# A gated mix of infinite attention and a spectral filter on one core: four-group score units, a semaphore between GpSimd and VectorE, whole gate exponentials, and a new written-out order

## The chip, the cores and the metric

The kernel runs on one core of a Trainium2 chip. The core has TensorE (PE, matrix multiplication into PSUM), VectorE (DVE), ScalarE (ACT), GpSimd (POOL), SyncE (SP, which issues most transfers) and 16 DMA engines. The metric is device microseconds of one execution; a kernel's time is the median of several runs. Lower is better.

## The reference

Two branches work on the same input x of 2048 tokens by 640 columns, in bf16, and a gate mixes them.

```
g = sigmoid((x * gate_w).sum(-1))                     # one number per token
a = attention(x) @ wo                                 # 32 heads of 20, 4 segments of 512 tokens
b = irfft2(rfft2(x) * (w_r + 1j*w_i))               # 2-D spectral filter over 2048 x 640
out = g*a + (1-g)*b
```

The mix is what the kernel returns; both branches read the same x. In attention, each segment of 512 tokens has causal softmax attention within itself, and from the second segment on also reads a memory: `phi(q) @ M / (phi(q) @ z)`, where `phi(t)` is `t+1` above zero and `exp(t)` elsewhere, and M and z sum `phi(k)^T v` and `phi(k)` of the segments before. A sigmoid of beta weighs the two per head.

## The kernel before

**Attention.** Heads are taken in eight groups of four, so that a head's 20 rows stand in a 32-row quarter of the PE array. A segment has four pairs of groups. Scores are computed transposed (keys on partitions) and only where the causal mask leaves something, in *units*: kind 0 is the first key block against 512 queries, kind 1 the second and third key block, kind 2 the rest (128 columns for each head of a group). A unit takes all four banks of the PSUM pool "qk"; there is one unit in those banks at a time. `qk_unit` (L1306) records the matmuls of a unit, one ScalarE exponential out of the four banks into the SBUF tile `ex` (L1343), and GpSimd `affine_select` operations that zero the masked corners (`mask`, L1361, recorded at L1364). `UNITS` lists, for each pair of groups, which units are made: kinds 0 and 1 for each group alone, kind 2 for both groups at once. `pv_flipped` (L1257) multiplies the values with a group's finished exponentials in the first three segments, `pv_group` does it in the last. `ex` has three slots of 5120 elements per partition, used in turn by the groups.

**Memory.** `mem_read_tile` (L1216) makes half a tile of 128 tokens: three matmuls of `phi(q)` with `Mz` into one PSUM bank, then on DVE a denominator (L1231), its reciprocal (L1234) and the multiplication out of PSUM (L1236, L1239 for the last segment). `dn` is a ring of four small buffers between these.

**Gate.** The gate's dot product is a 641st column of the value projection. `v_part` copies that one column from PSUM by DVE (L1192) into `gl`: one copy where the key order is plain, two of 64 partitions each where the halves are swapped. `gate` (L1073) then makes one ScalarE exponential of the four columns of a segment (L1080) and small operations after it.

**Spectral branch.** `fft` makes five matmul stages, F1, D, T, Tb and Db, with DVE multiplying by the weights between T and Tb (L1526). Db, the last (stationary tile Cp, moving tile big), makes 16 blocks in two parts each; DVE adds the parts into G (L1568).

**End.** `finish_tile` normalizes the stored attention (L1609), adds the memory part to it (L1617) and multiplies by `wo` and by the gate.

**The order.** Everything is first *recorded* as operations with what they read and write; nothing is emitted at that point. `ORDER`, a list of numbers written out in the file, then gives the order of all operations: number v means operation v // 2, on the first or second engine that it can run on, v % 2. It is made by a planner that is not in the file. `Sched.schedule` replays this list with a small model of times, only to choose PSUM banks and semaphores and to add the waits that follow from them; the order on each engine is the list's. `Sched.emit` turns dependences into semaphore waits. Each engine works its own list in order, so that an operation that waits holds up all behind it on its engine.

PE's 128 by 128 array can be divided: into column pieces of 64 or 32 (an operation recorded with mode -1 or -2 may be emitted whole or split into such pieces, by what stands before it; split matmuls have line L546, whole ones L548), into two row halves, or into four row quarters by two column halves, as scores use it. The planner's table `COST` charges for each change between such divisions.

DVE operations with two operands in SBUF, or in its fast modes, are recorded with `lock=True`: the planner takes them to use a port that GpSimd also uses. In its model a locked DVE operation begins when GpSimd is free, GpSimd begins when the locked operation ends, and with `TIE` a locked operation that had to wait loses some more time to the next mask. None of that is a wait in the emitted program: before, no semaphore orders the two engines for the port.

The SBUF is nearly full, which is why buffers are laid over others with `at=`.

Of the kernel before, what the change touches and what calls it, by code (L numbers as in the profile page):

```python
# [49 lines left out]
class Sched:  # L50
    HOP = 70.0
    TIE = 0.15
# [62 lines left out]
    def schedule(self, pools, order, nsem=56):  # L115
# [33 lines left out]
        tied = [False]  # L149
# [26 lines left out]
        def head(e):  # L176
# [22 lines left out]
            if e == "dve" and o.lock:  # L199
                tied[0] = free["pool"] > t  # L200
                t = max(t, free["pool"])
            elif e == "dve":
                tied[0] = False
            elif e == "pool":
                t = max(t, port)
            return t

        while len(self.order) < len(order):
# [38 lines left out]
            if e == "dve" and o.lock:  # L247
                port = t + occ
# [247 lines left out]
class Kern:  # L496
# [80 lines left out]
    def dma(self, dst, src, nbytes, r, w, prio, tr=False, name="", after=(), queue="sp"):  # L577
# [34 lines left out]
    UNITS = (((0,), 0), ((0,), 1), ((1,), 0), ((0, 1), 2), ((1,), 1))  # L612
# [121 lines left out]
    def alloc(self):  # L734
# [54 lines left out]
        self.xn = T("xn", [P, 4 * D], at=self.ex.off + 2 * 10240)  # L789
        self.on = T("on", [P, 4 * D])  # L790
        self.mem = T("mem", [P, 4 * D])
# [508 lines left out]
    def exo(self, s, g):  # L1300
        return ((s * 8 + g) % self.NEX) * 5120
# [389 lines left out]
```

## Time and profile before

| what | value |
|---|---|
| median of 3 runs | 247.91 us (247.44 to 248.65) |
| the profiled execution's own time | 248.49 us |
| its span, first to last instruction | 246.4 us |
| mean granted TensorE clock | 0.985 |
| instructions | 10962 |
| DMA | 40.99 MB, mean 166 GB/s |

The page gives for each engine its busy time, its share of the span and its instructions; then the span in 40 equal slices of 6.16 us, one digit each, which is the busy share in tenths (9 is 90% or more); "PEclk" is in the same way the granted share of the TensorE clock. The chain of work that ended last is followed back from the last instruction: at each step to what released it, or to the instruction before it on its engine. A row of a group of instructions has the line, the engine, the operation, output and inputs with their shapes, the count, then busy time in us and the mean of one in ns, then the engine's idle time ahead of them and what ended it. A row that has three numbers with slashes gives the shortest, median and longest duration of one instruction in ns. A row of the time line has the start, the length, the engine and line, and how many instructions were merged in it.

### The profile page before, as it was taken

To read this page: it belongs to the slowest core of one execution; us is meant where nothing else is said; L and a number is where in the kernel's file an instruction comes from. 1 tells how busy PE (TensorE), PEld (TensorE's weight loads), DVE (VectorE), ACT (ScalarE), POOL (GpSimd) and SP (SyncE) were. 2 spreads that over 40 slices of the span, in tenths; PEclk is the share of its full clock that TensorE was granted. 3 is DMA by queue.
4 is the path that set the end of the run, shared out by engine and by line. 5 is a ranking of instruction groups with operands and counts; after the bars stand their busy time and mean duration, and the time that the engine had idled before them with its cause. 6 is when DMAs were issued, how large, how long until landed. Compare 5 with 4: busy or idle time off the path is not lost.

```text
span 246.4 us, 10962 instructions
## 1 busy us (share of the span) xinstructions
PE 230.1 (93%) x4691; PEld 136.0 (55%) x4705; DVE 205.6 (83%) x492; ACT 195.0 (79%) x222; POOL 163.8 (66%) x287
## 2 busy tenths in 40 slices
PE   7999989999889999999999999998989999999993
PEld 3544546565544454565555455555534666666882
DVE  0499889899899999798989988999996879986562
ACT  2588875999899999999899988999886788866120
POOL 8435295697686283889489485583869869688520
PEclk9999999999999999999999999999995999999999
DMA  7999206849063976887877895783576967634424
GB/s 223 318 349 191 74 13 142 238 112 197 32 167 103 191 200 150 182 211 208 226 147 197 243 243 134 195 223 122 169 189 153 242 155 148 98 83 96 136 53 105
DMA packets 54251, 40.99 MB, mean 166 GB/s; under 512 B 25404, under 2 KB 52028, under 8 KB 54204
## 3 DMA queue, kind: packets, MB, share of 16 engines
q1 hardware_dynamic: 52156, 38.89, 64.1%
q10 hardware_dynamic: 2048, 1.41, 2.2%
q8 instruction: 37, 0.61, 1.1%
q14 instruction: 10, 0.08, 0.1%
HBM read 21.94 MB, written 11.12 MB: 134 GB/s over the span
## 4 chain that ended last, share of the span: by engine, by line
PE 66%; DVE 23%; issue 4%; ACT 3%; DMA 1%; ACTq 1%; SPq 0%; DVEq 0%
PE psum L548 43%; PE psum L546 23%; DVE UV L1526 4%; DVE oU L1617 2%; DVE mem L1236 2%; DVE Cp L560 2%; DVE G L1568 2%; ACT ex L1343 2%; DVE va L1194 1%; DMA qkp<-qk_scr 1%; DVE Ac L560 1%; DVE Bt L560 1%; DVE dn L1234 1%; DVE ub L560 1%; DVE gate L1192 1%
## 5 line engine op out<-in xcount | busy, mean ns | idle before, releaser
L1364 POOL TENSOR_SCALAR_AFFINE_SELECT ex<-ex 128x256 bf16<-128x256 bf16 (+2 forms) x224 | 123.3, 574 | 51.8 <-ACT ex L1343 49.4
L1343 ACT ACTIVATE ex<-psum 128x2048 bf16<-128x2048 f32 (+4 forms) x92 | 138.6, 1506 | 13.4 <-PE psum L548 11.5
L548 PE MATMUL psum<-qkp 20*64 20x64 bf16 (+5 forms) x1024 | 31.9, 268 | 1.4 <-ACT ex L1343 0.8
L548 PE MATMUL psum<-xT,wq 128*32 128x512 bf16 (+1 forms) x212 | 27.8, 380 | 0.5 <-ACT xT L558 0.2
L1526 DVE TENSOR_TENSOR UV<-psum,Wt 128x642 bf16<-128x642 f32 x32 | 25.1, 820 | 1.7 <-PE psum L548 1.5
L546 PE MATMUL psum<-wv,xT 128*32 128x321 bf16 (+3 forms) x320 | 23.0, 302 | 1.0 <-DVE pkn L1069 1.0
L548 PE MATMUL psum<-xT,wk 128*32 128x512 bf16 (+1 forms) x194 | 23.2, 380 | 0.3 <-issue 0.2
L546 PE MATMUL psum<-wo,oU 128*32 128x320 bf16 x480 | 23.1, 300 | 0.1
L548 PEld LDWEIGHTS psum<-qkp 20*64 20x64 bf16 (+1 forms) x1024 | 12.2, 101 | 17.9 <-ACT ex L1343 9.0
L548 PE MATMUL psum<-ex,va 128*32 128x512 bf16 (+4 forms) x480 | 17.1, 274 | 0.8 <-DVE UV L1526 0.4
L546 PE MATMUL psum<-big,Cp 128*32 128x321 bf16 (+1 forms) x300 | 17.3, 339 | 0.1
L1194 DVE TENSOR_TENSOR va<-psum,ebx 128x320 bf16<-128x320 f32 x32 | 15.3, 483 | 1.5 <-PE psum L548 0.7
L1568 DVE TENSOR_TENSOR G<-eo,psum 128x320 bf16<-128x320 f32 x32 | 14.9, 480 | 1.9 <-PE psum L548 0.8
L548 PE MATMUL psum<-tt,UV 128*128 128x128 bf16 (+1 forms) x192 | 15.7, 221 | 0.5 <-DVE mem L1236 0.2
L546 PEld LDWEIGHTS psum<-wv,xT 128*32 128x32 bf16 (+1 forms) x320 | 11.7, 102 | 7.2 <-issue 1.9
L548 PEld LDWEIGHTS psum<-ex,va 128*32 128x32 bf16 x480 | 10.6, 96 | 8.9 <-POOL ex L1364 1.9
L546 PEld LDWEIGHTS psum<-wo,oU 128*32 128x32 bf16 x480 | 12.5, 97 | 4.0 <-issue 1.1
L548 PEld LDWEIGHTS psum<-xT,wq 128*32 128x32 bf16 (+1 forms) x220 | 9.3, 96 | 9.7 <-issue 1.6
L548 PEld LDWEIGHTS psum<-tt,UV 128*128 128x128 bf16 (+1 forms) x192 | 11.9, 102 | 5.0 <-DVE qu L1012 0.6
L1155 ACT ACTIVATE et<-qu 128x1024 bf16<-128x1024 bf16 (+1 forms) x15 | 13.7, 910 | 0.5 <-DVE phq L1165 0.5
L548 PE MATMUL psum<-big,Ac 128*128 128x160 bf16 (+2 forms) x69 | 12.6, 258 | 1.4 <-DVE ub L560 0.5
L560 DVE CAST Cp<-psum 128x512 bf16<-128x512 f32 (+1 forms) x21 | 11.7, 582 | 2.3 <-PE psum L548 2.2
(119 smaller groups left out, 434.2 us busy)
## 6 DMA issues: line engine op xcount, KB each, us to landing
qkp<-qk_scr SPq DMA_DIRECT2D x24, 160.0 KB
tt<-tab_tt SPq DMA_DIRECT2D x8, 384.0 KB, 4.9
qk_scr<-qu SPq DMA_DIRECT2D x12, 256.0 KB, 3.1
u_scr<-ub SPq DMA_DIRECT2D x12, 256.0 KB, 3.4
Wt<-Wt SPq DMA_DIRECT2D x8, 321.0 KB, 4.2
xsb<-in_A_x_dram SPq DMA_DIRECT2D x8, 320.0 KB, 6.1
oU<-u_scr SPq DMA_DIRECT2D x15, 128.0 KB, 4.2
out_dram<-ot SPq DMA_DIRECT2D x38, 40.0 KB, 1.9
```

The source lines that it names most:

```text
L546: h = e.matmul(dst, wt, r_, start=st, stop=sp_, **{**kw, "tile_position": (0, q), "skip_group_check": True})
L548: h = e.matmul(o_, l_, r_, start=st, stop=sp_, **kw)
L560: alts["dve"] = (lambda e: e.tensor_copy(dst(), src()), 67 + 1.04 * n, 68.0)
L1155: self.one("act", lambda e: e.activation(et.ap(0, [1, m]), src(), ACT.Exp), m, both, [b("et")], late, after=[b("ets", q) for q in range(2) ...
L1192: self.one("dve", lambda e, p0=p0, p1=p1, n=n: e.tensor_copy(self.gl.ap(4 * s + i, [1, 1], p0=p0, np_=n), self.ps(bank, 320, [1, 1], p0=p1 ...
L1194: self.one("dve", lambda e: e.tensor_tensor(va.ap(i * H * VW + h0 * VW, [VW, nh], [1, DH]), self.ps(bank, 0, [DH, nh], [1, DH]), self.ebx. ...
L1236: fn = lambda e: e.tensor_tensor(self.mem.ap(i * D + 64 * q, [4, 16], [P, 5], [1, 4]), self.ps(bank, 0, [VW, 16], [4, 5], [1, 4]), dn.ap(1 ...
L1343: self.one("act", lambda e, d=d, q=q: e.activation(self.ex.ap(*d), self.ps(bank, *q), ACT.Exp, scale=SC), n, [bank], [self.exb(s, 2 * pr + ...
L1364: self.one("pool", lambda e: e.affine_select(self.ex.ap(e0 + d0, [1280, 4], [1, n], np_=np_), self.ex.ap(e0 + s0, [1280, 4], [1, n], np_=np_),
L1526: self.one("dve", lambda e, rh=rh, UV=UV, Wt=Wt, gp=gp, bank=pb[rh]: e.tensor_tensor(UV.ap(rh * 644, [322, 2], [1, KD]), self.ps(bank, 0, ...
L1568: self.one("dve", lambda e, q=q, n2=n2, bank=bank, eo=eo: e.tensor_tensor(self.G.ap(n2 * D + 639 * q, [1 - 2 * q, 320]), eo.ap(q, [1, 320] ...
L1617: self.either(lambda e: e.tensor_tensor(oT.ap(a * P, [L, 5], [1, P]), oT.ap(a * P, [L, 5], [1, P]), mT.ap(0, [P, 5], [1, P]), ALU.add), D, ...
```

## The change

Seven edits, the last of which moves nearly everything a little:

- Kind-2 score units are made once for four groups, in the first three segments (`UNITS`); the last segment keeps the old units (`UNITS3`). The kind-2 part of `ex` gets four slots of its own behind the three slots of the other parts (`exo`, `pitch`, `exb`); the last segment uses the old layout over the same bytes, with waits on what it overlays (`exbefore`).
- In the planner's replay, the first GpSimd operation after a locked DVE operation gets a dependence on it, if it would begin less than 800 ns after that operation's end. That is a semaphore wait in the emitted program. `TIE` is gone.
- The gate's column goes straight from PSUM through a ScalarE exponential of 128 partitions by one column for each token tile; two DVE copies for each segment swap the halves afterwards.
- `dn` and `rs` have two buffers instead of four.
- The float buffer `dnr` lies over the second `ub` buffer, and `gT` on eight partitions behind the third chunk of `Cp`.
- The first transposes of x, whose tile `xn` lies over the end of `ex`, hold fewer parts of it.
- `ORDER` is a new list.

```diff
-    TIE = 0.15
...
             if e == "dve" and o.lock:
-                tied[0] = free["pool"] > t
                 t = max(t, free["pool"])
-            elif e == "dve":
-                tied[0] = False
             elif e == "pool":
                 t = max(t, port)
...
-            if e == "dve" and tied[0] and pos["pool"] < len(queue["pool"]):
-                q = queue["pool"][pos["pool"]]
-                if all(p.t1 is not None and p.t1 + self.HOP <= t + 30.0 for p in q.preds) and free["pool"] <= t + 1.0:
-                    t += self.TIE * q.alts["pool"][1]
+            if e == "pool" and porter is not None:
+                if t < port + 800.0:
+                    o.dyn.append(porter)
+                porter = None
...
             if e == "dve" and o.lock:
-                port = t + occ
+                port, porter = t + occ + lat + self.HOP, o
...
-    UNITS = (((0,), 0), ((0,), 1), ((1,), 0), ((0, 1), 2), ((1,), 1))
+    UNITS = ((((0,), 0), ((0,), 1), ((1,), 0), ((1,), 1), ((0, 1, 2, 3), 2)), (((0,), 0), ((0,), 1), ((1,), 0), ((1,), 1)))
+    UNITS3 = (((0,), 0), ((0,), 1), ((1,), 0), ((0, 1), 2), ((1,), 1))
...
-        self.ex = T("ex", [P, self.NEX * 4 * 1280])
+        self.ex = T("ex", [P, self.NEX * 4 * 1088 + 4 * 768])
...
-        self.dnr = T("dnr", [P, P], F32)
+        self.dnr = T("dnr", [P, P], F32, at=self.ub[1].off)
...
-        self.gT = T("gT", [P, P], F32)
+        self.gT = T("gT", [P, P], F32, at=self.Cp.off + 20480)
...
-        self.rs = [T(f"rs{i}", [P, 32], F32) for i in range(4)]
-        self.dn = [T(f"dn{i}", [P, 32], F32) for i in range(4)]
+        self.rs = [T(f"rs{i}", [P, 32], F32) for i in range(2)]
+        self.dn = [T(f"dn{i}", [P, 32], F32) for i in range(2)]
...
-        self.one("act", lambda e: e.activation(sl(self.gr), sl(self.gl), ACT.Exp, scale=-1.0), 4,
-                 [b("gl", s, i, p0) for i in range(4) for p0 in ((0, 64) if i % 2 else (0,))], [b("gr", s)], prio, fix=190, name="gate_exp")
+        for p0 in (0, 64):
+            self.one("dve", lambda e, p0=p0: e.tensor_copy(self.gr.ap(c0 + 1, [2, 2], p0=64 - p0, np_=64), self.gx.ap(c0 + 1, [2, 2], p0=p0, np_=64)), 2,
+                     [b("gr", s, 1), b("gr", s, 3)], [b("gx", s, p0)], prio, fix=120, name="gate_cp")
...
-            for p0, p1, n in ((64, 0, 64), (0, 64, 64)) if i % 2 else ((0, 0, P),):
-                self.one("dve", lambda e, p0=p0, p1=p1, n=n: e.tensor_copy(self.gl.ap(4 * s + i, [1, 1], p0=p0, np_=n), self.ps(bank, 320, [1, 1], p0=p1, np_=n)),
-                         1, [bank], [b("gl", s, i, p0)], prio, name="gate_cp")
+            gt = self.gx if i % 2 else self.gr
+            self.one("act", lambda e: e.activation(gt.ap(4 * s + i, [1, 1]), self.ps(bank, 320, [1, 1]), ACT.Exp, scale=-1.0), 1, [bank],
+                     [b("gr", s, i)], prio, fix=190, name="gate_exp")
...
-            for u, parts in enumerate(self.UNITS):
-                self.qk_unit(s, pr, u, parts)
+            units = self.UNITS[pr % 2] if s < 3 else self.UNITS3
+            for u, parts in enumerate(units):
+                self.qk_unit(s, pr, u * 5.0 / len(units), parts)
...
     def exb(self, s, g, k):
-        return self.b("ex", (s * 8 + g) % self.NEX, k)
-
-    def exo(self, s, g):
-        return ((s * 8 + g) % self.NEX) * 5120
+        if s == 3:
+            return self.b("ex3", g % self.NEX, k)
+        return self.b("exc", g % 4, k) if k in ("c0", "m3") else self.b("ex", (s * 8 + g) % self.NEX, k)
+
+    def exo(self, s, g, o=0):
+        if s == 3:
+            return g % self.NEX * 5120 + o
+        return 13056 + g % 4 * 768 + o - 1088 if o >= 1088 else ((s * 8 + g) % self.NEX) * 4352 + o
+
+    def pitch(self, s, o):
+        return 1280 if s == 3 else 192 if o >= 1088 else 1088
```

`ORDER` has 2328 numbers before and 2312 after and is left out here. Of the operations that can run on two engines, the new list puts some on the other one: fewer large SBUF operations on GpSimd, and a somewhat different split of PSUM copies between DVE and ACT.

More of the change, by code (lines that the diff above doesn't have):

```diff
@@ L787, in alloc @@
         self.NEX = 3
-        self.ex = T("ex", [P, self.NEX * 4 * 1280])
-        self.xn = T("xn", [P, 4 * D], at=self.ex.off + 2 * 10240)
+        self.ex = T("ex", [P, self.NEX * 4 * 1088 + 4 * 768])
+        self.xn = T("xn", [P, 4 * D], at=self.ex.off + 2 * 8704)
         self.on = T("on", [P, 4 * D])
@@ L803, in alloc @@
         self.ebx = T("ebx", [P, 3 * H], F32)
-        self.gr, self.g1, self.gl = (T(f"gate{i}", [P, 16], F32) for i in range(3))
+        self.gr, self.g1, self.gx = (T(f"gate{i}", [P, 16], F32) for i in range(3))
         self.gg = T("gg", [P, 32], F32)
-        self.gT = T("gT", [P, P], F32)
+        self.gT = T("gT", [P, P], F32, at=self.Cp.off + 20480)
         self.omh = T("omh", [P, 64])
         self.ebg = T("ebg", [P, 4 * H], F32)
-        self.rs = [T(f"rs{i}", [P, 32], F32) for i in range(4)]
-        self.dn = [T(f"dn{i}", [P, 32], F32) for i in range(4)]
+        self.rs = [T(f"rs{i}", [P, 32], F32) for i in range(2)]
+        self.dn = [T(f"dn{i}", [P, 32], F32) for i in range(2)]
         print("SBUF", self.cur, self.top)
@@ L915, in x_turn @@
                     items.append((th, P))
-                self.mms(items, [b("xn", i), b("fcat"), bank] + [self.exb(0, 2, k) for k in ("a0", "b0", "b1", "c0", "m1", "m3")], [], -0.9, name="turn", mode=0)
+                self.mms(items, [b("xn", i), b("fcat"), bank] + [self.exb(0, 2, k) for k in ("a0", "b0", "m1")], [], -0.9, name="turn", mode=0)
             self.Sc.op(self.copy_alts(lambda c=c: self.xT[0].ap(c * L, [1, L]), lambda bank=bank: self.ps(bank, 0, [1, L]), L),
@@ L1101, in gate @@
         self.mms(items, [b("hi", s), b("lo", s), b("fcat"), bank], [], prio + 4.0, name="gateT", mode=2)
-        self.one("dve", lambda e: e.tensor_copy(self.gT.ap(0, [1, 8], [8, 16], np_=8), self.ps(bank, 0, [16, 8], [1, 16], np_=8)), P, [bank], [b("gT")],
+        self.one("dve", lambda e: e.tensor_copy(self.gT.ap(0, [1, 8], [8, 16], p0=96, np_=8), self.ps(bank, 0, [16, 8], [1, 16], np_=8)), P, [bank], [b("gT")],
                  prio + 4.0, name="gate_ops")
         for x in range(2 if s < 3 else 1):
-            self.dma(lambda x=x: dap(self.gd.ap(), (2 * s + x) * L, [8, 4], [32, 16], [1, 8]), lambda x=x: self.gT.ap(0, [8, 16], [1, 8], p0=4 * x, np_=4),
+            self.dma(lambda x=x: dap(self.gd.ap(), (2 * s + x) * L, [8, 4], [32, 16], [1, 8]), lambda x=x: self.gT.ap(0, [8, 16], [1, 8], p0=96 + 4 * x, np_=4),
                      4 * 512, [b("gT")], [b("gd", s, x)], prio + 4.0, name="st_g")
@@ L1289, in denominators @@
                  [b("gd", s, 1)], [b("gcc")], prio, name="ld_gc")
-        self.one("dve", lambda e: e.reciprocal(self.dnr.ap(0, [1, P]), self.dnc.ap(0, [1, P])), P, [b("dnc")], [b("dnr")], prio, per=7.0,
+        self.one("dve", lambda e: e.reciprocal(self.dnr.ap(0, [1, P]), self.dnc.ap(0, [1, P])), P, [b("dnc")], [b("ub", 1, 0), b("ub", 1, 1)], prio, per=7.0,
                  name="den_rec")
         self.one("dve", lambda e: e.tensor_tensor(self.rc.ap(0, [1, P]), self.dnr.ap(0, [1, P]), self.gcc.ap(0, [1, P]), ALU.mult), P,
-                 [b("dnr"), b("gcc")], [b("rc"), b("dnc")], prio, name="den_gate")
+                 [b("ub", 1, 0), b("ub", 1, 1), b("gcc")], [b("rc"), b("dnc")], prio, name="den_gate")
         self.dma(lambda: dap(self.rd.ap(), s * H * L, [P, P], [1, P]), lambda: self.rc.ap(0, [1, P]), P * P * 2,
@@ L1297, in exb, with exbefore @@
     def exb(self, s, g, k):
-        return self.b("ex", (s * 8 + g) % self.NEX, k)
-    def exo(self, s, g):
-        return ((s * 8 + g) % self.NEX) * 5120
+        if s == 3:
[7 more added lines that the diff above has]
+        return 1280 if s == 3 else 192 if o >= 1088 else 1088
+    def exbefore(self, s, g):
+        if s < 3 or g >= self.NEX:
+            return []
+        end = (g + 1) * 5120
+        old = [self.exb(2, q, k) for q in (5, 6, 7) if self.exo(2, q) < end and self.exo(2, q) + 4352 > g * 5120 for k in ("a0", "b0", "m1")]
+        return old + [self.exb(2, q, k) for q in (4, 5, 6, 7) if self.exo(2, q, 1088) < end and self.exo(2, q, 1088) + 768 > g * 5120 for k in ("c0", "m3")]
     def exall(self, s, g):
@@ L1328, in qk_unit @@
         ks = "abc"[kind]
-        e0, step = self.exo(s, g), self.exo(s, g + 1) - self.exo(s, g) if kind == 2 else 0
+        e0, step = self.exo(s, g), self.exo(s, g + 1) - self.exo(s, g) if s == 3 else 0
+        sp = self.pitch(s, 0)
         sh = self.SH23[s == 3]
         if kind == 0 or (kind == 1 and s < 3):
-            outs = [((e0 + 576 * kind, [1280, 4], [1, 512]), (0, [512, 4], [1, 512]))]
+            outs = [((e0 + 576 * kind, [sp, 4], [1, 512]), (0, [512, 4], [1, 512]))]
         elif kind == 1:
@@ L1343, in qk_unit @@
             self.one("act", lambda e, d=d, q=q: e.activation(self.ex.ap(*d), self.ps(bank, *q), ACT.Exp, scale=SC), n, [bank],
-                     [self.exb(s, 2 * pr + (n_ if kind == 2 and s == 3 else gp), ks + str(n_ * (kind == 1))) for gp in gps], prio - self.QK_LEAD, name="exp" + str(n_)[n_ == 0:])
+                     [self.exb(s, 2 * pr + (n_ if kind == 2 and s == 3 else gp), ks + str(n_ * (kind == 1))) for gp in gps], prio - self.QK_LEAD, name="exp" + str(n_)[n_ == 0:],
+                     after=[q for gp in gps for q in self.exbefore(s, 2 * pr + gp)])
         for gp in gps:
```

17 lines of the change are left out of this document (8 added, 9 removed), and 194 rows, old and new, of the table ORDER.

## Prediction

> **What bounds the kernel now.** I read the page first (busy shares, the slices, the chain), then windows cut where the clock changes, then the chain inside them.
>
> ```profile
> PE 230.1 (93%) x4691; PEld 136.0 (55%) x4705; DVE 205.6 (83%) x492; ACT 195.0 (79%) x222; POOL 163.8 (66%) x287
> POOL 8435295697686283889489485583869869688520
> PEclk9999999999999999999999999999995999999999
> PE 66%; DVE 23%; issue 4%; ACT 3%; DMA 1%; ACTq 1%; SPq 0%; DVEq 0%
> ```
>
> TensorE (PE) is the bound, with VectorE (DVE) next to it: the chain of work that ended last is two thirds PE and a quarter DVE, and only 4% of it is waiting that nothing explains. So an edit counts by its PE time times about 0.66, its DVE time times about 0.23, and hardly at all if it is on ScalarE (ACT, 3%) or GpSimd (POOL, none). The clock row has one 5 among the nines. These are the windows around it (start:end, length, then busy time and count for PE, weight loads, DVE, ACT and POOL, then the granted clock):
>
> ```profile
> 177.66:181.08 3.42, 3.37 (x110) 1.75 (x99) 3.30 (x10) 2.97 (x6) 2.80 (x6) 1.00 0.90 203
> 181.08:184.49 3.41, 2.51 (x44) 1.09 (x40) 3.35 (x14) 2.83 (x2) 2.18 (x4) 1.00 0.49 163
> 184.49:187.90 3.41, 3.41 (x60) 1.55 (x56) 2.67 (x8) 2.61 (x3) 2.99 (x4) 0.50 0.85 201
> 187.90:191.32 3.42, 3.42 (x44) 1.55 (x37) 1.60 (x4) 1.96 (x4) 2.87 (x5) 0.50 0.55 129
> 191.32:194.73 3.41, 3.01 (x89) 2.12 (x86) 3.07 (x13) 2.37 (x4) 2.66 (x6) 1.00 0.93 291
> ```
>
> For 6.83 us PE runs at half clock and is busy in every moment of it, while DVE and ACT run dry. The window ahead of it is thin: 44 matmuls against 110, and PE idle for 3.41 - 2.51 = 0.90 us. What fills that thin window is in the chain (start, length, what) and in the groups of the window:
>
> ```profile
> 181.27 0.43 DVE eo L560
> 181.70 0.39 DVE mem L1239
> 183.06 0.41 DVE mem L1239
> 183.86 1.81 PE psum L546 x27
> 186.26 3.61 PE psum L546 x50
> ...
> L548 PE MATMUL psum<-Mz,phq 128*128 128x154 bf16 (+1 forms) x12 | 1.4, 225 | 0.7 <-DVE mem L1239 0.4 <-DVE eo L560 0.3
> ```
>
> Four memory-read tiles (three short matmuls each) stand almost behind each other, each waiting for a PSUM bank that DVE empties. In the order of the program before, three of the last segment's eight tiles follow each other directly and the fourth comes after a score unit of 12 matmuls alone.
>
> **The change, part by part.** The sum is made against the profiled execution: span 246.4 us, its own time 248.49, which is 0.58 above the median 247.91. I subtract from the median.
>
> *1. New order: the thin window.* In the built program after, two of the eight tiles are adjacent at most; all other neighbours have at least one inverse-transform or value matmul group between them. So the thin window should fill and the half clock should not follow. At full clock PE's work of 6.83 us takes 3.41, but the other engines must do theirs too: ACT 2.61 + 1.96 = 4.57 us in these two windows. Bounds are 0 and -3.4; I take 6.83 - 4.57 = **-2.3**. Of the 0.90 us of idle PE I take **-0.5** (bounds 0 and -0.9). By the Trainium skill, page "TensorE: Matmul & The Clock Gate", section "HAM oscillation — how this bites in real kernels", the clock falls back only after an idle gap of about 3.4 us. The row above disagrees: PE was busy 2.51 of 3.41 us and the clock fell all the same. By that page an order that only fills short gaps gains nothing here; that is rival A below.
>
> *2. Changeovers of the array's tiling.* Counting the order, PE changes between whole-array, 32-column, 64-column, 64-row and score tilings 231 times before and 216 times after (12 small score units become 6). The price from four starts:
>
> ```profile
> 196.74 0.31 PE L546 MATMUL psum<-wo,oU 128*32 128x320 bf16 x4
> 196.88 0.45 PE L546 MATMUL psum<-big,Cp 65*32 65x321 bf16 x8
> 197.15 0.31 PE L546 MATMUL psum<-wo,oU 128*32 128x320 bf16 x4
> 197.40 0.40 PE L548 MATMUL psum<-qkp 20*128 20x320 bf16 x8
> ```
>
> The same four matmuls hand over after 196.88 - 196.74 = 0.14 us to their own tiling and after 197.40 - 197.15 = 0.25 to another: 0.11 per changeover. 15 x 0.11 = 1.65, times 0.66: **-1.1** (0 to -1.65). Splitting whole matmuls into column pieces changes elsewhere, but the columns streamed are the same: nothing.
>
> *3. GpSimd waits for VectorE.* A DVE operation on two SBUF operands and GpSimd's masks exclude each other. Rows: time of one (min/median/max), then two places.
>
> ```profile
> L1165 DVE TENSOR_TENSOR phq<-phq,et x9: 417/682/1561, 45.1 to 175.2; 128x1024 bf16<-128x1024 bf16 x6, 128x512 bf16<-128x512 bf16 x3
> L1609 DVE TENSOR_TENSOR oU<-oU,r x13: 362/415/571, 180.2 to 211.1; 128x512 bf16<-128x512 bf16 x13
> L1617 DVE TENSOR_TENSOR oU<-oU,mT x4: 727/1111/1970, 212.4 to 226.0; 128x640 bf16<-128x640 bf16 x4
> 74.64 1.56 DVE L1165 TENSOR_TENSOR phq<-phq,et 128x1024 bf16<-128x1024 bf16 x1
> 73.77 2.96 POOL L1364 TENSOR_SCALAR_AFFINE_SELECT ex<-ex 128x512 bf16<-128x512 bf16 x5
> 224.09 2.84 DVE L1617 TENSOR_TENSOR oU<-oU,mT 128x640 bf16<-128x640 bf16 x2
> 223.01 4.24 POOL L1364 TENSOR_SCALAR_AFFINE_SELECT ex<-ex 128x512 bf16<-128x512 bf16 x7
> ```
>
> At 74.64 the operation takes 1.56 against a median of 0.68: several masks pass ahead of it, +0.88. At 224.09 two additions take 2.84; at the smallest seen, 0.727, they take 1.45: +1.39. Both are on the chain. With the new semaphore wait the next mask cannot pass; the one already running still can, half a mask (4.24 / 7 / 2 = 0.3) for each of three operations. 0.88 + 1.39 - 0.9 = **-1.4** (0 to -2.3). By the Trainium skill, page "SBUF — State Buffer", section "Who interferes with whom", whoever issues first holds the port pair for one whole instruction; read as one mask's delay at most, it would leave nothing to save here, and 2.84 us for two additions speaks against that reading.
>
> The price: masks now queue behind the waiting one on POOL, and value matmuls wait for masks. The order has 67 waits of POOL on DVE where there were 17, so 50 more. POOL's row has a 9 in 6 of 40 slices: 50 x 6 / 40 = 7.5 waits fall where POOL has no slack; at 0.415 each that is 3.1 us, and I take a quarter: **+0.8** (0 to the rival's price).
>
> *4. Score units of four groups, gate, moved work.*
>
> ```profile
> L1343 ACT ACTIVATE ex<-psum 128x2048 bf16<-128x2048 f32 x56 | 105.2, 1878 | 10.1 <-PE psum L548 9.1
> L1343 ACT ACTIVATE ex<-psum 128x1024 bf16<-128x1024 f32 x12 | 12.2, 1020 | 0.3 <-PE psum L548 0.2
> L1192 DVE COPY gate<-psum x24: 145/157/161, 33.3 to 166.0; 64x1 f32<-64x1 f32 x16, 128x1 f32<-128x1 f32 x8
> L1080 ACT ACTIVATE gate<-gate x4: 197/197/206, 41.7 to 166.2; 128x4 f32<-128x4 f32 x4
> L1012 DVE CAST qu<-psum x20: 407/414/427, 46.2 to 174.3; 128x256 bf16<-128x256 f32 x20
> L560 DVE CAST Cp<-psum 128x512 bf16<-128x512 f32 x13 | 8.6, 684 | 1.3 <-PE psum L548 1.3
> L1617 POOL TENSOR_TENSOR oU<-oU,mT x4: 1391/1400/1427, 203.7 to 217.8; 128x640 bf16<-128x640 bf16 x4
> ```
>
> Exponentials: 12 x 1.020 - 6 x 1.878 = 0.97 us less ACT, hidden at 3% of the chain; 0. If that cover were gone it is worth 1. The six big units stand in the order right behind the last value matmuls whose buffer they overwrite, on PE itself, so no new wait of size. The gate: DVE loses 24 x 0.157 = 3.8 and gains 8 small copies, not in the trace, at the same 0.157 = 1.3 (0 to 0.4 each, by the two ends of L1192 and L1012): 2.5 us less, times 0.23 = **-0.5** (0 to -2.5). ACT gains 16 x 0.2 - 0.8 = 2.4, hidden. Moved work: DVE takes over 6 PSUM copies net, 0.414 to 0.684 each, so 2.5 to 4.1, and two additions from POOL (1.4 us there); three smaller ones go the other way. About 3 us, times 0.23 = **+0.7** (0 to +3). The smaller dn and rs rings and the buffers laid over others reuse tiles far apart in the order: 0.
>
> **Sum:** -2.3 - 0.5 - 1.1 - 1.4 - 0.5 + 0.7 + 0.8 = -4.3. Median 247.91 - 4.3 = **243.6 us** (span 242.1).
>
> **The rivals.**
>
> *A. The half clock stays.* For it: other windows are thin as well, and a new order may thin one of them:
>
> ```profile
> 61.61:65.03 3.42, 2.52 (x87) 1.57 (x74) 2.96 (x7) 3.33 (x3) 3.35 (x9) 1.00 0.15 49
> 68.44:71.85 3.41, 2.76 (x88) 1.61 (x85) 2.89 (x7) 3.38 (x4) 3.41 (x8) 1.00 0.73 135
> ```
>
> At 61.61 PE is as little busy (2.52) and the clock held, so what counts is not busy time alone and I cannot compute the margin; against it, the tiles that made the thin stretch are spread. Without -2.3 and -0.5: 247.91 - 1.5 = 246.4. (The skill's idle-gap rule gives this time too.)
>
> *B. POOL becomes late: the slower side.* Place: masks in front of the value matmuls. 18 of 40 slices have POOL at 8 or 9 tenths, so 50 x 18 / 40 = 22 waits; if each sends 0.415 us to the end, 9.1 us in place of 0.8: 247.91 - 5.1 + 9.1 = 251.9; at half of that 247.4. It decides from 5.1 / 50 = 0.1 us of each added wait reaching the end. For it: POOL is full (3.41 of 3.41) at 68.44. Against it: over the run POOL has 246.4 - 163.8 = 82.6 us idle.
>
> *C. DVE takes PE's place.* It is at 83% and gets nothing net off. Then parts 1 and 2 give nothing: -1.4 - 0.5 + 0.7 + 0.8 = -0.4, 247.5. Against it: in the half-clock windows DVE is idle 2.6 of 6.8 us.
>
> **How the numbers follow.** Forecast 0.52, A 0.20, B 0.20, C 0.08. A measurement of this kernel tells about 0.5% (1.2 us) from no change. The forecast is faster; of A 0.13 is faster and 0.07 the same; of B 0.15 slower, 0.02 the same, 0.03 faster; of C 0.02, 0.05 and 0.01 slower. Together faster 0.70, same 0.14, slower 0.16. The forecast with most terms at their good end (-3.4 - 0.9 - 1.65 - 2.3 - 0.5 + 0.7 + 0.8) is 240.7; the range runs from 240.8 to 249.6, which covers A, C and the lower half of B and leaves about 0.1 at each end.
>
> **What would show it.** Right: a clock row with no 5 around 180 to 195, and the memory-read tiles of the last segment spread; no DVE addition over 1.3 us at L1617's successor; score units of 48 matmuls with no wait over 0.5 us; POOL idle mostly behind ACT still. Wrong: a half-clock window anywhere (A), POOL waits on DVE in the chain with PE behind masks (B), DVE's chain share over 35% (C).

## The result and the profile after

On the chip the changed kernel took 246.95 us (median of 20 runs, 243.57 to 252.42) against 249.00 for the kernel before (20 runs, 246.53 to 252.25): ratio 0.9881, 95% interval 0.9843 to 0.9919, about 2.9 us less. This ratio and those below compare only the runs within about 1.5% of the fastest of their kernel (11 of these 20 after), so it is not the quotient of the two medians, which lie 2.05 us apart. Run again in the first experiment the changed kernel took 245.98 us (6 runs), ratio 0.9861 (0.9801 to 0.9921). The lines of after are those of that second profile (243.24 us, span 241.4); the first profiled run took 247.56.

From its page: busy time of each engine, two rows of the slices, and the shares of the chain of work that ended last.

```profile
PE 226.8 (94%) x4661; PEld 135.6 (56%) x4674; DVE 201.6 (83%) x482; ACT 193.2 (80%) x222; POOL 155.9 (65%) x287
POOL 8236567676886686718884855982669956677610
PEclk9999999999999999999999999999999999999998
PE 61%; DVE 15%; DMA 11%; ACT 5%; SPq 3%; issue 2%; POOL 1%; DVEq 0%
```

PE is 3.3 us less busy than the 230.1 of before and idle for 14.6 us where it was 16.3. Half of the 6.83 us at half clock is 3.4, so nothing else of PE's work got shorter. (Both traces lack some matmul records, 4661 here for 4674 weight loads.) The clock row has no 5 within the run. DVE's part of the chain fell from 23% to 15%, POOL is not late (1%). New in the chain are transfers and SP's queue: 14% together, where before had 1%.

Two lines whose predecessors the prediction quoted (shortest, median, longest duration in ns):

```profile
L1163 DVE TENSOR_TENSOR phq<-phq,et x9: 410/683/965, 46.1 to 171.9; 128x1024 bf16<-128x1024 bf16 x6, 128x512 bf16<-128x512 bf16 x3
```

```profile
L1632 DVE TENSOR_TENSOR oU<-oU,mT x6: 480/520/749, 205.8 to 218.3; 128x640 bf16<-128x640 bf16 x6
```

The longest of the first was 1561 and is 965; the longest addition was 1970 and is 749. What GpSimd waits for (us in total, times, longest), first before, then after:

```profile
POOL ex L1364 <- ACT ex L1343: 49.4, 31, 5.2
POOL xf L947 <- DVE xf L947: 6.3, 2, 4.9
```

```profile
POOL ex L1379 <- ACT ex L1358: 17.1, 9, 4.6
POOL ex L1379 <- ACT gate L1190: 6.8, 3, 5.7
POOL ex L1379 <- DVE oU L1624: 4.6, 4, 1.8
POOL ex L1379 <- DVE xsb L949: 4.3, 4, 1.9
```

Of the waiting behind score exponentials 32 us are gone, 6.8 of waiting behind the gate's exponentials are new, and small waits behind many VectorE operations stand in their place (all of them together some 45 us, where before had 15.5). GpSimd's idle time was there, and the new waits took it over.

One more number matters below. A stretch of 3.41 us at half clock lowers the mean granted clock of a run by 0.7%, so a run's mean tells whether it had one (below 0.9955) or not. Of the 69 executions of before beside the experiments, 27 had none; they took 247.9 us on average, the other 42 249.1. Of the 26 executions of after, 13 had none; they took 245.3, the others 248.3. Without any half clock the new kernel is thus 2.6 us faster, so the half clock is not where the gain comes from. The 3.0 us between the two kinds of executions of after are not the price of the half clock alone, because what thins a stretch also costs time: the first profiled run had no half clock and yet took 247.56.

### The profile page after: what moved, and what is told of

The parts are those of the page before. It is cut to its first block, busy times and chain, and to the rows that moved or that the text cites. A ratio compares the mean times of both kernels' runs of the same rounds, so it can differ in the third digit from the quotient of the medians.

```text
span 245.7 us, 10937 instructions
## 1 busy us (share of the span) xinstructions
PE 230.5 (94%) x4674; PEld 136.4 (56%) x4674; DVE 201.0 (82%) x482; ACT 193.3 (79%) x222; POOL 156.2 (64%) x287
## 3 DMA queue, kind: packets, MB, share of 16 engines
q10 hardware_dynamic: 1952, 1.33, 2.0%
## 4 chain that ended last, share of the span: by engine, by line
PE 58%; DMA 15%; DVE 15%; ACT 4%; issue 3%; SPq 2%; POOL 1%; POOLq 0%
PE psum L544 36%; PE psum L542 22%; DMA xsb<-in_A_x_dram 5%; DMA oU<-u_scr 5%; ACT ex L1358 3%; SPq L579 2%; DMA mT<-o_scr 2%; DVE Ac L556 2%; DVE UV L1541 2%; DMA g_scr<-gT 1%; DVE Bt L556 1%; DMA fcat<-tab_fcat 1%; DVE qkp L556 1%; DVE ub L556 1%; DVE oU L1624 1%
## 5 line engine op out<-in xcount | busy, mean ns | idle before, releaser
L1379 POOL TENSOR_SCALAR_AFFINE_SELECT ex<-ex 128x256 bf16<-128x256 bf16 (+2 forms) x224 | 118.0, 550 | 57.8 <-ACT ex L1358 16.3
L1358 ACT ACTIVATE ex<-psum 128x2048 bf16<-128x2048 f32 (+3 forms) x86 | 137.5, 1599 | 17.8 <-PE psum L544 16.3
L544 PE MATMUL psum<-qkp 20*64 20x64 bf16 (+5 forms) x1024 | 31.1, 266 | 2.1 <-ACT ex L1358 1.0
L544 PE MATMUL psum<-xT,wq 128*32 128x512 bf16 (+1 forms) x220 | 29.6, 380 | 0.6 <-ACT xT L554 0.2
L542 PE MATMUL psum<-wv,xT 128*32 128x321 bf16 (+3 forms) x400 | 26.9, 301 | 0.0
L544 PE MATMUL psum<-xT,wk 128*32 128x512 bf16 (+1 forms) x195 | 21.7, 380 | 0.2
L542 PEld LDWEIGHTS psum<-wv,xT 128*32 128x32 bf16 (+1 forms) x400 | 13.8, 100 | 6.3 <-issue 2.2
L949 POOL TENSOR_TENSOR xsb<-xf 128x320 bf16<-128x320 bf16 (+2 forms) x13 | 9.9, 766 | 9.5 <-DVE xf L944 4.4
L556 DVE CAST ot<-psum 128x320 bf16<-128x320 f32 x22 | 10.2, 488 | 5.6 <-DMA out_dram<-ot 2.4
L556 DVE CAST Ac<-psum 128x512 bf16<-128x512 f32 x18 | 11.8, 684 | 1.9 <-PE psum L542 1.6
```

The costliest lines, as they stand in the source:

```text
L542: h = e.matmul(dst, wt, r_, start=st, stop=sp_, **{**kw, "tile_position": (0, q), "skip_group_check": True})
L544: h = e.matmul(o_, l_, r_, start=st, stop=sp_, **kw)
L556: alts["dve"] = (lambda e: e.tensor_copy(dst(), src()), 67 + 1.04 * n, 68.0)
L949: self.either(lambda e, dst=dst, src=src, d0=d0, n=n, op=op: e.tensor_tensor(xs.ap(o + dst, [D, 2], [1, n]), xf.ap(src + d0, [321, 2], [1, ...
L1358: self.one("act", lambda e, d=d, q=q: e.activation(self.ex.ap(*d), self.ps(bank, *q), ACT.Exp, scale=SC), n, [bank], [self.exb(s, 2 * pr + ...
L1379: self.one("pool", lambda e: e.affine_select(self.ex.ap(self.exo(s, g, d0), [self.pitch(s, d0), 4], [1, n], np_=np_), self.ex.ap(self.exo( ...
```

## The experiments

Two explanations stand against each other. By the prediction the gain is mostly the clock and the changeovers, and the waits are a small term (-1.4 + 0.8). By the other the gain is that GpSimd can no longer pass a waiting VectorE operation, and the other parts give little or cost. The first fell with the second run below. Ratios are to the runs of before on the same chip; 0.01 is 2.5 us.

### The changed kernel again, the waits taken out, and the waits alone

The changed kernel without an edit, for more times and a second profile:

> The changed kernel once more, for a second profile and for more times with their clocks. Theory 1 (the gain is the missing half-clock stretch plus cheaper changeovers and shorter waits at the shared port): executions whose mean clock is 0.996 or more take about 245.5 us, those with a half-clock stretch about 3 us more; about half of the executions have none, against few of the kernel before; ratio to before 0.985 to 0.992. Rival (the half clock has nothing to do with the gain): executions with and without a stretch differ by less than 1 us.

Measured 245.98 us, ratio 0.9861 (0.9801 to 0.9921): as in the result. The three executions without a half clock took 244.1 us on average, the three others 247.2. So a half clock goes with some 3 us, and half of the executions have none, both as expected; but of before 9 of 23 had none as well, which is not few.

The waits out of the new plan:

```diff
             if e == "pool" and porter is not None:
-                if t < port + 800.0:
-                    o.dyn.append(porter)
                 porter = None
```

> The changed kernel with GpSimd's added waits on VectorE taken out (18 of 67 waits stay, the ones that data need), all else and the whole order the same. Theory 1 puts 1.4 us of gain against 0.8 us of cost on these waits, so this should be 0.5 to 1.5 us slower than the changed kernel: ratio to before 0.990 to 0.995, with locked VectorE additions of up to 2 us in the profile again. Rival (the waits cost GpSimd more than they save): 1 us faster than the changed kernel, ratio 0.983 or less.

Measured 254.91 us (253.89 to 255.68), ratio 1.0253 (1.0211 to 1.0295). The interval is far from the one with the waits: 0.0372 of 248.5 are **9.2 us**, three times the whole gain and far beyond the 0.6 that the prediction's two terms leave. The time line at the worst place, VectorE and GpSimd without the waits (start, length, engine and line, number merged):

```profile
115.44 2.48 DVE L1161 TENSOR_TENSOR phq<-phq,et 128x1024 bf16<-128x1024 bf16 x1
117.84 1.31 DVE L1160 TENSOR_SCALAR phk<-qu 128x1024 bf16<-128x1024 bf16 x1
```

```profile
113.49 6.58 POOL L1377 TENSOR_SCALAR_AFFINE_SELECT ex<-ex 128x256 bf16<-128x256 bf16 x12 [0.48 <-ACT gate L1188]
```

And with them, the same operations:

```profile
111.75 0.82 DVE L1163 TENSOR_TENSOR phq<-phq,et 128x1024 bf16<-128x1024 bf16 x1
112.49 0.41 DVE L1162 TENSOR_SCALAR phk<-qu 128x1024 bf16<-128x1024 bf16 x1
```

Twelve masks of 0.55 us follow each other without a gap, and the two operations need 3.7 us in place of 1.2. Behind them in VectorE's order stands the copy that empties a PSUM bank for PE. The windows there (length, busy PE, weight loads, DVE, ACT, POOL, granted clock):

```profile
116.54:119.95 3.41, 1.15 (x23) 0.67 (x19) 3.41 (x4) 3.03 (x4) 3.41 (x7) 1.00 0.60 166
119.95:123.37 3.42, 3.42 (x44) 1.82 (x46) 3.35 (x7) 0.71 (x1) 0.55 (x2) 0.50 0.44 106
```

PE does 1.15 us of work in 3.41, and the next window is granted half the clock: one late operation is paid for twice. All six runs had a half-clock stretch. Over the run, the ten large groups of VectorE operations that read and write SBUF alone take 55.3 us without the waits and 43.8 with them.

The waits alone, in the old order (the same replacement of `TIE` by `porter` as in the change; GpSimd's waits for VectorE go from 17 to 60):

> The kernel before with the added waits alone (60 waits of GpSimd on VectorE in place of 17), same order and operations. Theory 1: 0.5 to 1.4 us faster, ratio 0.994 to 0.998; the operation that took 1.56 us at 74.6 us takes about 1.0, the two additions of 2.84 us about 2. Rival: the waits hold up masks and it is 1 to 4 us slower, ratio 1.004 to 1.016.

Measured 247.14 us, ratio 0.9930 (0.9898 to 0.9962), 1.7 us less. The ten groups go from 51.3 to 43.1 us here, 8.2 us, and the four additions that the prediction quoted from 1.23 to 0.76 us each, but only 1.7 us reach the end. That the old order has less of these operations on its path would explain it; that was not measured. The sign holds in both orders, and the size depends on the order.

The waits of the first 45 us only taken out, 11 of 50:

```diff
-                if t < port + 800.0:
+                if 45000.0 < t < port + 800.0:
```

> The new plan with the added waits of GpSimd for VectorE left out only before 45 us of the plan (about 11 of 50); the rest stay. The run without any of them took some 9 us more than the new kernel, and its chain of waits shows at 30.6 to 36.6 us two key-feature operations of 0.9 us and others stretched by masks, after which TensorE is 2.7 us later than in the new kernel. Theory (each wait pays on the spot where a VectorE operation on the chain would be overtaken, and nothing is given back later): +2.0 to +3.0 us over the new kernel, ratio about 0.996 to 1.000. Rival (the loss in the first stretch is slack that later waits absorb; the 9 us come from the half clock and the end of the kernel): within 0.7 us of the new kernel. Rival (the waits only help together): most of the 9 us come back, ratio above 1.01.

Measured 249.30 us, ratio 1.0011 (0.9972 to 1.0050): 3.2 us over the new kernel by the ratio of the result, a little above the expected 2.0 to 3.0. The intervals are about 1 us wide on each side: both rivals are out, and the time fits waits that pay one by one where they stand.

### The thin window

The window before the half clock of before is filled: four memory-read tiles do their matmuls four times, the result of the computation stays the same.

```diff
             items.append((th, nh * VW))
+        if s == 3 and 2 * i + q in (0, 2, 5, 6):
+            items = items * 4
```

> The kernel before with the matmuls of four memory-read tiles of the last segment (the ones close to each other) made four times over into the same bank, the last time being the one that counts: about 0.5 us of useless TensorE work for each of the four, 2 us in all, where TensorE was idle for 0.9 us. If array use in that stretch decides the clock (theory 1), the half clock near 184 us goes in most executions and the kernel is 0.5 to 1.5 us faster in spite of the work: ratio 0.994 to 0.998. If the order only matters through waits (rival), the clock stays at 0.985 and it is 1 to 2 us slower: ratio 1.004 to 1.008.

Measured 247.24 us, ratio 0.9964 (0.9922 to 1.0006). Ten of 12 runs had no half clock, against 9 of 23 of before in that job. So more use of PE in this stretch does keep the clock in most executions. The time is 0.9 us less, not 2.8, and its interval reaches no change. The same tiles moved apart in the order instead:

```diff
-Db21 memrd18 memrd21 memrd16 qk65 memrd22 Db22 Db23 Db45 Db46 Db42 Db43 Db44 qk62
+Db21 memrd18 qk65 Db22 Db23 memrd16 Db45 Db46 Db42 Db43 Db44 memrd21 qk62
 ...
-Db60 Db61 Db62 Db30
+Db60 Db61 Db62 memrd22 Db30
```

> The kernel before with three memory-read tiles of the last segment moved between groups of the last inverse transform; nothing else. My first term in full (half clock and idle TensorE gone): 2.8 us less, ratio 0.989. What the filled stretch gave (0.9 us at the same place): ratio 0.994 to 0.998, with the share of runs above a clock of 0.995 rising from 9 of 23 to over two thirds. Rival (moving them delays the tiles that the output needs): ratio 1.000 to 1.005.

Measured 248.74 us, ratio 1.0009 (0.9972 to 1.0045): nothing; 5 of 12 runs without half clock, against 14 of 29 of before in that job. The expectation failed in all its forms but the rival's. Spreading did not fill the stretch: in the profiled run PE is busy 2.19 and 2.33 us of two windows near 180 and 187 us (rows in the last section), less than the 2.51 of before. And the reverse, four tiles put together in the new order:

```diff
-Db12 Db24 memrd18 Db3 ... Db45 memrd19 Db46 ... Db31 memrd20 memrd21 Db32
+Db12 Db24 Db3 ... Db45 Db46 ... Db31 memrd18 memrd19 memrd20 memrd21 Db32
```

> The new plan with four memory-read tiles of the last segment put directly behind each other, as they stood before; same work. If the spread of these tiles is what keeps the clock (my first term): mean granted clock of most runs below 0.994 with a half-clock stretch near 181 to 190 us, and +1.0 to +3.3 us over the new kernel, ratio 0.990 to 0.999. Rival (VectorE bounds this stretch and the order within it does not matter): clock as in the new kernel's runs, time within 0.7 us of it, ratio 0.984 to 0.990.

Measured 247.14 us, ratio 0.9956 (0.9921 to 0.9991): 1.9 us more than the new kernel. All 12 runs had a half clock. Windows of the profiled run:

```profile
188.03:191.44 3.41, 1.33 (x14) 0.72 (x13) 2.25 (x8) 1.59 (x1) 3.41 (x7) 1.00 1.51 289
191.44:194.85 3.41, 3.41 (x56) 2.21 (x57) 2.94 (x12) 2.49 (x3) 2.19 (x5) 0.50 0.94 177
194.85:198.27 3.42, 3.42 (x67) 2.13 (x67) 3.34 (x12) 1.61 (x3) 1.35 (x3) 0.50 1.06 151
```

Four tiles together do bring the stretch of 6.83 us back. (This run has a second one of 3.41 us at 157.31, behind another thin window.) The old order has three together, and its clock fell in 42 of 69 executions; where it fell in those without a profile is not known.

### Changeovers

The groups of the transforms that the plan tiles in column pieces by choice take the whole array, 66 changeovers more, after all else has been planned:

```diff
         self.nsem = nsem
+        for o in pe:
+            if o.mode == -1 and o.name in ("D", "Db"):
+                o.emode = 0
```

> The new plan with all else as it is, but the groups of the first and the last inverse transform that the plan tiles in column pieces next to column-tiled neighbours take the whole array instead: 66 changeovers more (281 for 215), 189 matmuls fewer, same columns streamed. If a changeover costs the 0.11 us that I took from four starts and TensorE bounds most of the time: 66 x 0.11 = 7.3 us of TensorE, times 0.61 to 1, +4.4 to +7.3 us over the new kernel, ratio about 1.005 to 1.017. Rival (a changeover costs nothing beyond what the smaller number of matmuls gives back, so the 16 saved ones gave nothing): within 1 us of the new kernel, ratio 0.985 to 0.992.

Measured 253.71 us, ratio 1.0167 (1.0103 to 1.0230): 7.1 us over the new kernel by the ratios; between runs without half clock (two of the six here) 251.0 - 245.3 = 5.7. Its page:

```profile
PE 239.4 (94%) x4440; PEld 134.5 (53%) x4440; DVE 201.5 (79%) x482; ACT 194.3 (76%) x222; POOL 156.2 (61%) x287
```

This trace lacks no matmul record, so it is compared with traces that lack none and have no half clock within the run. The first two are of the new plan (the first profile of after, and the run with a load moved that follows below), the third is of the old order with the tiles spread:

```profile
PE 230.5 (94%) x4674; PEld 136.4 (56%) x4674; DVE 201.0 (82%) x482; ACT 193.3 (79%) x222; POOL 156.2 (64%) x287
PE 229.8 (94%) x4674; PEld 135.8 (56%) x4674; DVE 202.3 (83%) x482; ACT 193.0 (79%) x222; POOL 157.2 (65%) x287
PE 228.9 (93%) x4651; PEld 134.5 (55%) x4651; DVE 206.4 (84%) x492; ACT 194.8 (79%) x222; POOL 164.0 (67%) x287
```

PE is busy 8.9 to 9.6 us more than in the first two, of which 5.1 are the half of a stretch of 10.24 us at half clock; the other 3.8 to 4.5 are 0.06 to 0.07 us of busy PE for each changeover. By the times, 5.7 / 66 to 7.1 / 66 = 0.09 to 0.11 us of each reaches the end, close to the price that I took. The rival is out; what makes up the rest of the price is not shown.

### The gate

The gate's exponentials whole, in the old order: 16 exponentials of one column where the first copy of each tile stood, 8 small copies where the 4 exponentials stood (the change's own lines).

> The old order with the gate's exponentials taken whole from PSUM by ScalarE (16 of one column, 8 small copies on VectorE) in the place of 24 copies on VectorE and 4 exponentials. My term: -0.5 us (0 to -2.5), ratio 0.990 to 1.000. Rival (ScalarE's 16 short operations stand in front of score exponentials and PSUM banks come free later): 0 to +1 us, ratio 1.000 to 1.004.

Measured 252.36 us (251.04 to 252.99), ratio 1.0168 (1.0120 to 1.0215): **4.2 us slower**, past the rival's own bound. The chain of its profiled run from 117.62 (start, length, what), and a row of its waits:

```profile
117.62 1.88 ACT ex L1344
119.50 0.07 ACT gate L1193
119.57 0.02 issue
119.59 0.49 DVE va L1195
120.09 1.19 DVE Cp L560 x2
```

```profile
DVE va L1195 <- ACT gate L1193: 4.4, 6, 1.5
```

The exponential of one column stands in ScalarE's queue behind a score exponential of 1.88 us. The value multiplication of the same PSUM bank waits for it, then VectorE's copies, then PE. The windows there show PE thin and then at half clock, and all six runs had a half clock (13 of 17 of before's in that job):

```profile
118.77:122.18 3.41, 1.88 (x26) 0.75 (x25) 2.52 (x7) 1.93 (x4) 1.74 (x3) 1.00 0.95 215
122.18:125.59 3.41, 3.41 (x62) 1.52 (x63) 2.02 (x4) 1.69 (x3) 0.88 (x2) 0.50 0.42 90
```

In the new kernel no value multiplication waits for the gate:

```profile
L1192 DVE TENSOR_TENSOR va<-psum,ebx x32: 469/488/492, 31.5 to 166.3; 128x320 bf16<-128x320 f32 x32
its engine sat idle before it (us, times) until:
  PE psum L542: 1.3, 5
```

### A load that the new order moved

The 819 KB load of the output weights (800 KB in the units of the profile, in which a row load has 128) goes from the place ahead of the row loads to one behind the last of them:

```diff
 SP, in order:
-ld_wo1 ld_wo20 pad22 ld_u1 ld_u13 oT0 ... ld_u10 ld_r2 ld_u11 oT5
+ld_wo1 pad22 ld_u1 ld_u13 oT0 ... ld_u10 ld_r2 ld_u11 ld_wo20 oT5
```

> The new plan with one load moved: the 819 KB copy of the output weights that is first read near 229 us stands in the SP queue directly ahead of the loads of the inverse transform's rows (oU); it goes behind the last of them. In the new kernel's trace the chain runs through such a load of 7.30 us (median 3.2) from 181.19, and in the runs with a lower clock PE then waits 1.4 to 3 us and the next window is thin. Theory (this moved transfer is a price that my sum left out): the slow landings go, fewer runs with a half-clock stretch than 13 of 26, 1.0 to 2.5 us less than the new kernel, ratio to before 0.978 to 0.984. Rival (the load is late for another reason, the queue of SP itself): within 0.7 us of the new kernel, ratio 0.985 to 0.991.

Measured 244.50 us (242.60 to 247.67), ratio 0.9836 (0.9786 to 0.9887); 5 of 6 runs had no half clock. The transfers of oU, issue to landing in us, in the new kernel (two rows of the tile's view), in its first profiled run, and with the load moved:

```profile
L579 SPq DMA_DIRECT2D oU<-u_scr x15: 513/569/1393, 172.2 to 200.3; - x15
DMA to landing us min/median/max: 2.6/3.2/7.1
```

```profile
DMA to landing us min/median/max: 2.6/3.2/8.1
```

```profile
DMA to landing us min/median/max: 2.5/3.1/3.7
```

The slow landing is gone: five profiles of the new plan with the load in its old place have 7.0 to 8.1 us for the slowest row load, this one 3.7. In the first profiled run PE had waited for the operation behind it:

```profile
PE psum L542 <- DVE oU L1624: 1.4, 1, 1.4
```

With the load moved PE's waits have no such row. That the large load made the rows land late is shown; the gain in time (1.1 us by the ratios) lies within the intervals. With the small load moved some 25 us earlier too:

> As the run before it, and the 164 KB load of output weights ahead of the same loads is moved some 25 us earlier as well, where its buffer is already free. Theory: at least as fast as with the large load alone moved, 0 to 0.7 us less. Rival (earlier it delays loads of weights and twiddles near 150 us that PE needs): slower than that run by up to 1 us.

Measured 246.16 us, but with runs from 242.02 to 250.63 and a ratio of 0.9773 (0.9701 to 0.9846): not to be told from the run before it (the ratio rests on two runs). 5 of 6 had no half clock.

### Both single edits in the old order

> The old order with both of the single edits together: GpSimd's waits for VectorE, and the four memory-read tiles with their matmuls done four times. If the two gains are separate: -1.7 - 0.9 = -2.6 us, ratio 0.987 to 0.992, as much as the whole new plan. Rival (the waits thin another stretch and the clock falls there, as at 61.9 us in the run with the waits alone): no better than the waits alone, ratio 0.991 to 0.997.

The edits are the two shown above, the waits alone and the filled window, in one kernel. Measured 246.38 us (12 runs), ratio 0.9919 (0.9883 to 0.9955), 2.0 us less; none of 12 runs had a half clock. The ratio lies in the ranges of both expectations, and its interval holds both the sum and the waits alone. Two small edits of the old order come within 1 us of the whole new plan.

## Why the prediction was right, and where it was not

The direction was right and the time, 246.95, lies in the range; the forecast of -4.3 us was too much by 1.4 against the 2.9 of the ratio. That it came so near is luck. The waits, forecast at -0.6 with their price, are worth -9.2 in the new order; all the rest, forecast at -3.7, comes out at +6.3. Two errors of 8.6 and 10.0 us cancelled.

- **Step 1, half clock -2.3 and idle PE -0.5, is the step that failed.** That a thin stretch brings the clock down holds: with it filled, 10 of 12 executions kept the clock (12 of 12 with the waits too), and with four tiles together none of 12 did. Two things were wrong. The 6.83 us were those of one execution: the clock stayed up in 27 of 69 executions of before. And an order that spreads these tiles does not keep the clock: the new plan has a half clock in 13 of 26 executions (neither of its profiles fell on one, so where is not known), and spreading the tiles in the old order changed nothing. In the mean over all executions the half clock goes with 42/69 x (249.1 - 247.9) = 0.7 us before and 13/26 x (248.3 - 245.3) = 1.5 after. The change did not win this term; it lost 0.8 on it.
- **Step 2, changeovers -1.1.** By the times the price of 0.11 is about right, and of it 0.8 to 1 reaches the end where the sum had 0.66, so 15 changeovers would be worth 1.3 to 1.6 us by these times. No run shows that saving itself: without half clock PE is busy 228.9 us in the old order with its tiles spread and 229.8 to 230.5 in the new plan.
- **Step 3, waits -1.4 with a price of +0.8.** The sign is right and the reading of the rows too: several masks pass ahead of one operation. The size is wrong. I summed the two stretched rows that lay on the chain of before; in the old order the waits are worth 1.7 net, in the new one 9.2. That term cannot be read from the trace of before; that the new order was laid out as if GpSimd could not pass is the likely reason, and was not tested apart. The price of +0.8 cannot be told apart from the gain, but little of it is seen: PE waits 0.6 us for masks, where before had 0.4, and GpSimd's idle time took the waits. By the Trainium skill, page "SBUF — State Buffer", section "Who interferes with whom", an engine holds the shared ports for one instruction; the 2.48 us of an operation that takes 0.68 in the median fits GpSimd being the next holder again, several times in a row.
- **Step 4, units 0, gate -0.5, moved work +0.7.** The units alone were not tried. The gate's -0.5 has the wrong sign in the old order (+4.2): I counted 2.4 us more ACT work as hidden, and did not ask what stands ahead of each short exponential in ScalarE's queue. The new order leaves no such wait for the value multiplication; what the gate costs or saves there was not measured. Among the moved work I left out the 819 KB load ahead of the row loads.
- **Rival A** (half clock stays) came true in half of the executions. Its -1.5 us lies as near to the measured -2.9 as the forecast's -4.3, but it too left the waits at -0.6. **B** did not come: POOL is 1% of the chain, PE waits 0.6 us for masks. **C** did not: DVE's share fell to 15%.
- Of the signs that I named, "POOL idle mostly behind ACT" was wrong: 17.1 us behind score exponentials and 6.8 behind the gate's, some 45 behind VectorE. The others of one execution held: no addition over 0.75 us, and PE's longest wait for a score exponential was 0.4 us. The clock row without a 5 was a weak sign: it says nothing of the next execution.

What stays open: without the waits the new plan is 6.3 us slower than before (1.0253). The gate (4.2 in the old order), the moved load, the more exposed VectorE operations (55.3 us for 51.3) and the half clock in all six runs each point that way; how much each takes in the new order was not separated. So the runs show that the new plan gains only with its waits, and not what it loses without them.

## What to carry to other kernels

A written-out order and its semaphores are one design: price a wait in the order that it is made for, since the same wait was worth 1.7 us in one order and 9.2 in the other. Before a stall at a lowered clock goes into a sum, look at the mean clock of every run, because one trace does not tell how often it happens. When an operation moves to another queue, read what stands ahead of it there, for short operations (0.17 us behind 1.88) and for loads (800 KB ahead of a 128 KB row load) alike.

The fastest kernel of these runs is the changed one with the large load moved: 244.50 us, 0.9836 of before (0.9786 to 0.9887).

## What the runs showed of the hardware that was not expected

- In these profiles the clock fell in whole windows of 3.41 us (3.41, 6.83 or 10.24), each time after a window in which PE was thinly used: busy 2.51 (before), 1.15 (waits out), 1.33 (tiles together) and 1.88 us (gate) of 3.41, as shown above, and here 1.73 and 2.65 (the waits alone in the old order, and more changeovers):

```profile
61.88:65.30 3.42, 1.73 (x37) 0.96 (x31) 2.25 (x5) 2.54 (x3) 2.28 (x5) 1.00 0.00 0
65.30:68.71 3.41, 3.41 (x37) 1.66 (x36) 1.60 (x6) 1.30 (x2) 1.11 (x2) 0.50 0.02 5
```

```profile
198.86:202.27 3.41, 2.65 (x75) 1.74 (x67) 2.16 (x7) 2.67 (x4) 0.43 (x2) 1.00 0.58 161
202.27:205.68 3.41, 3.39 (x58) 2.01 (x59) 3.36 (x12) 1.71 (x1) 2.05 (x4) 0.50 0.58 160
```

  Busy time alone does not decide. The window at 61.61 of before, quoted in the prediction, held at 2.52, and so did thinner ones: these of the first profile of after, of the waits and the filled window together, and two of the spread tiles:

```profile
190.80:194.21 3.41, 2.05 (x64) 1.18 (x60) 1.77 (x7) 1.56 (x5) 1.79 (x4) 1.00 0.77 174
60.75:64.16 3.41, 1.95 (x55) 1.34 (x56) 2.53 (x6) 3.32 (x3) 3.07 (x7) 1.00 0.16 54
180.11:183.52 3.41, 2.19 (x67) 1.07 (x63) 3.34 (x12) 2.84 (x3) 2.97 (x6) 1.00 0.71 184
186.94:190.35 3.41, 2.33 (x23) 1.13 (x22) 3.27 (x9) 2.08 (x4) 3.34 (x6) 1.00 0.98 147
```

  What separates them in these traces is how much of the array the matmuls use. An estimate from their shapes, rows times columns times streamed columns, against the 16 whole-array matmuls of 512 columns that fit in 3.41 us at the 0.21 us between their starts: the seven windows just ahead of a fall reach 0.18 to 0.37, and of some 930 others at full clock none is below 0.35. That is a reading of 14 traces, not a test.

  The same kernel has the stretch in one execution and not in the next (42 of 69 had it), which fits windows whose phase to the program varies; that was not tested. By the Trainium skill, page "TensorE: Matmul & The Clock Gate", section "HAM oscillation — how this bites in real kernels", it is an idle gap longer than about 3.4 us that brings the clock down. The window at 198.86 disagrees as the prediction's row did: PE was busy 2.65 of 3.41 us.
- A VectorE operation that wants the port took 1.8 us more than its median (2.48 for 0.68) while GpSimd's masks of 0.55 us ran back to back, the time of more than three of them.
